# The last two experts' first product as seven block products, in a reordered tail

## The chip, the cores and the metric

One core of a Trainium2 chip runs the whole program. The metric is the device time of one execution in microseconds (us); the time of a kernel is the median of its runs. Engines are named as in the profile: PE is TensorE (its weight loads are PEld), DVE is VectorE, ACT is ScalarE, POOL is GpSimd, SP is SyncE, which only issues transfers here. PSUM is the memory that PE accumulates in, SBUF the one that holds operands.

## The reference

An attention over 4 x 8 heads of 768 positions and 64 elements comes first: queries and keys are assigned to 16 clusters, a query sees the keys of its own cluster, and the result is gathered into x with 3072 rows of 512. Then a mixture of 8 experts, with 384 rows for each:

```
logits = x @ w_gate                     # 3072 x 8
order = np.argsort(-logits.flatten())   # greedy: best pair first
# a row goes to an expert if the row is free and the expert has under 384 rows
for e in range(8):
    h = np.maximum(x[mask_e] @ w1[e], 0.0)   # 384 x 512 @ 512 x 1024
    out[mask_e] = h @ w2[e]                  # 384 x 1024 @ 1024 x 512
```

The first product and the second of an expert have the same number of multiplications. Everything that the change touches is the first product of two experts.

## The kernel before, in words

**Order.** The steps of the program stand in two tables of text, `ATT_ORDER` (line 21) for the attention and `FFN_ORDER` (line 181) for the experts. A step is a name and numbers, `hid,5,2,0,1`, and the loop at line 1503 calls the function `f_hid(5, 2, 0, 1)` for it. Each engine runs its own instructions in the order in which the table issues them, and waits on semaphores for operands that other engines write. No loop and no scheduler decides anything beyond the table.

**Precision.** A number is kept as two fp16 parts, an upper part and a lower part (what is left of it). A product is three PE passes: upper by upper, upper by lower, lower by upper.

**An expert p.** Its rows are ranked and picked: `rank` (1294) is a product on PE that counts the marks `mk` made by `gt` and `ge` (1283) on DVE; `scan`, `addr`, `stt0`, `pm`, `ph`, `pl`, `ohl`, `ohh`, `ohv` (1298 to 1351) turn the counts into one-hot tiles on DVE; `col` (1358, three products on PE), `pb0`, `pb1` (DVE), `rep` (1369, PE), `pi` and `idx` (1372, 1375, DVE) give the list of 384 rows. `gx` (1422, POOL) gathers 128 rows by that list and `xt` (1426, SP) transposes them into `xgt`; there are three of each. `es2`, `upe`, `lt`, `upd` (1312 to 1321) take the rows out of the scores for the next expert.

**Its weights.** `w_load` (1394, 1397, SP) brings w1 and w2 in eight pieces of 512 KB into `wr`; for each piece `wsc` (1408) scales it and `whi` (1411) takes the upper half on ACT, and `wlo` (1418) subtracts to get the lower half on POOL, each 128x1024 elements.

**Its products.** `hid` (function `triple`, 1450) makes the first product: 8 row blocks of the hidden layer x 4 blocks of the depth x 3 passes = 96 matmuls, each of 128x128 weights by 128x384 columns. Each finished block of 128x384 in PSUM goes through `rel` (1479, ACT, relu and upper half `hh`) and `hlo` (1482, DVE, lower half `hl`). `out` (1492) makes the second product: 3 groups of 128 rows x 8 x 3 = 72 matmuls of 512 columns (expert 7's third group is cut into 384 and 128 columns). `oev` (1496, ACT) copies a group out of PSUM and `sc` (1499, POOL) scatters it to the result. `hid` and `out` share five PSUM buffers, all called `pf`.

Before the change the products of experts 5, 6 and 7 follow each other whole: 96 `hid`, then 72 `out`, for each expert. Work for the next expert's rows and weights is strewn between them.

## Time and profile before

| | us |
|---|---|
| runs | 675.21, 675.34, 676.72 |
| median | 675.34 |
| the profiled execution | 676.28 |
| its span | 674.5 |
| PE busy | 634.6 (94%) |
| POOL busy | 514.3 (76%) |
| DVE busy | 500.0 (74%) |
| ACT busy | 420.8 (62%) |

The span is the time between the first and the last record of the trace; what the execution takes beyond it (676.28 - 674.5) lies outside. Busy shares are means over the whole span: attention and experts have different limits, so the stretch that the change touches has to be looked at by itself. The mean granted clock of PE over the span is 0.979 of its upper level. A matmul's busy time includes the way through the array and overlaps the next one; what a matmul costs in a row of matmuls is the distance from its start to the next start.

### The profile page before, as it was taken

The page shows a single profiled execution, that of the slowest core. Times are in us where ns is not written, and L with a number is a line of the kernel's source. Part 1 is how long each engine was busy: PE and PEld are TensorE (multiplying, and loading weights), DVE is VectorE, ACT ScalarE, POOL GpSimd, SP SyncE. Part 2 cuts the span into 40 slices and gives each one's busy share as a digit, 9 for nine tenths or more (in the row PEclk, how much of TensorE's full clock was granted, in tenths as well). Part 3 has the DMA queues.
Part 4 walks back from the last instruction along what each step waited for, and adds up shares of the span by engine and source line. Part 5 has one row for each costly group of instructions (what it writes and reads, how often), then busy time and mean ns, then how long its engine had stood idle before and what let it go on. Part 6 is the DMA issues. An engine that isn't in the chain of part 4 may idle for free. (4 is left out here: it accounts for less than half of the span.)

```text
span 674.5 us, 19513 instructions
## 1 busy us (share of the span) xinstructions
PE 634.6 (94%) x8154; PEld 427.0 (63%) x8154; DVE 500.0 (74%) x1092; ACT 420.8 (62%) x558; POOL 514.3 (76%) x451
## 2 busy tenths in 40 slices
...
GB/s 233 144 144 194 204 171 215 135 164 196 197 131 161 201 143 114 149 91 74 28 28 97 25 171 172 284 96 280 203 191 223 181 231 161 242 297 212 47 1 48
DMA packets 175451, 105.85 MB, mean 157 GB/s; under 512 B 135426, under 2 KB 160002, under 8 KB 175362
## 3 DMA queue, kind: packets, MB, share of 16 engines
...
q14 instruction: 25, 0.20, 0.1%
...
## 5 line engine op out<-in xcount | busy, mean ns | idle before, releaser
L841 POOL TENSOR_TENSOR rt<-pt 128x768 f16<-128x768 f32 x180 | 277.6, 1563 | 27.3 <-ACT pt L833 26.5
L833 ACT ACTIVATE pt<-sc 128x768 f32<-128x768 f32 x192 | 149.8, 811 | 93.6 <-PE sc L830 74.6
L791 DVE TENSOR_REDUCE mxs<-sc 128x1 f32<-128x768 f32 x192 | 176.0, 950 | 17.7 <-PE sc L787 17.2
L1450 PE MATMUL pf<-xgt,w1h 128*128 128x384 f16 (+1 forms) x640 | 130.1, 295 | 0.4 <-DVE xgt L751 0.4
L855 PE MATMUL av<-vh,rt 128*128 128x65 f16 x1152 | 120.6, 193 | 1.8 <-POOL rt L841 1.7
L852 PE MATMUL av<-vh,pt 128*128 128x65 f16 x1152 | 120.7, 194 | 1.1 <-DVE xb L885 1.1
L854 PE MATMUL av<-vl,pt 128*128 128x64 f16 x1152 | 120.4, 192 | 0.0
L854 PEld LDWEIGHTS <-pt 128*128 128x128 bf16 x1152 | 105.7, 98 | 8.9 <-issue 1.8
L852 PEld LDWEIGHTS <-pt 128*128 128x128 bf16 x1152 | 106.2, 97 | 7.4
L855 PEld LDWEIGHTS <-rt 128*128 128x128 f16 x1152 | 105.3, 97 | 2.1 <-POOL rt L841 2.0
L826 PE MATMUL sc<-qbt,kbt 99*128 99x384 f16 x384 | 94.5, 327 | 1.3 <-DVE mxs L791 0.7
L830 PE MATMUL sc<-qat,kat 128*128 128x384 f16 x384 | 94.5, 327 | 0.0
L787 PE MATMUL sc<-kbt,qbt 80*128 80x384 f16 x384 | 89.5, 327 | 2.8 <-ACT qbt L749 0.6
L1450 PE MATMUL pf<-xgt,w1l 128*128 128x384 f16 (+1 forms) x320 | 89.6, 294 | 0.0
L1408 ACT ACTIVATE wr<-wr 128x1024 f32<-128x1024 f32 x64 | 66.7, 1046 | 28.3 <-DVE cs L1344 20.8
L1450 PEld LDWEIGHTS <-w1h 128*128 128x128 f16 x640 | 58.0, 98 | 29.9 <-DVE xgt L751 1.0
L1492 PE MATMUL pf<-w2l,hh 128*128 128x512 f16 (+2 forms) x200 | 73.5, 370 | 0.0
L1492 PE MATMUL pf<-w2h,hl 128*128 128x512 f16 (+2 forms) x200 | 73.4, 370 | 0.0
L1492 PE MATMUL pf<-w2h,hh 128*128 128x512 f16 (+2 forms) x200 | 73.3, 370 | 0.0
L1418 POOL TENSOR_TENSOR w1l<-wr,w1h 128x1024 f16<-128x1024 f32 x32 | 67.4, 2133 | 4.5 <-ACT w1h L1411 4.3
L1418 POOL TENSOR_TENSOR w2l<-wr,w2h 128x1024 f16<-128x1024 f32 x32 | 67.7, 2138 | 3.9 <-ACT w2h L1411 3.5
L1482 DVE SCALAR_TENSOR_TENSOR hl<-pf,hh 128x384 f16<-128x384 f32 x56 | 30.9, 553 | 46.4 <-ACT hh L1479 46.0
...
## 6 DMA issues: line engine op xcount, KB each, us to landing
...
xg<-xrow,idx POOLq DMA_INDIRECT x24, 6.8
```

The source lines that it names most:

```text
L787: nc.tensor.matmul(p[:, half, :S // 2], QBT[u][:D + C, i, :], KBT[u][:D + C, h * J + half * 3:h * J + half * 3 + 3, :], start=True, stop=True)
L791: nc.vector.tensor_reduce(mxs[u % 3][:, i:i + 1], MP.pop((u, i))[:, :, :S // 2], axis=AX.XY, op=OP.max)
L826: nc.tensor.matmul(ps[:, half, :S // 2], KBT[u][:ER + 3, s, :], QBT[u][:ER + 3, cs, :], start=True, stop=False)
L830: nc.tensor.matmul(ps[:, half, :S // 2], KAT[u][:, s, :], QAT[u][:, cs, :], start=False, stop=True)
L833: nc.scalar.activation(pts[(u * 12 + s // 2) % RP][:, s % 2], MP.pop((u, "b", s))[:, :, :S // 2], AF.Exp, scale=ESC)
L841: (nc.vector if e == "D" else nc.gpsimd).tensor_sub(rts[x][:, s % 2], p.rearrange("p a b -> p (a b)"), hi_view(pts[x])[:, s % 2])
L852: nc.tensor.matmul(o[:, j, :D + 1], hi[:, js], VH[u][:, s, :D + 1], start=(kt == 0 and j == 0), stop=False, skip_group_check=True)
L854: nc.tensor.matmul(o[:, j, :D], hi[:, js], VL[u][:, s, :], start=False, stop=False, skip_group_check=True)
L855: nc.tensor.matmul(o[:, j, :D + 1], r[:, js], VH[u][:, s, :D + 1], start=False, stop=(kt == J - 1), skip_group_check=True)
L1418: nc.gpsimd.tensor_sub(lo, wrs[c], hi)
L1450: nc.tensor.matmul(o, (w1l if i == 2 else w1h)[x][:, c, fs], xgt[x][:, h + int(i == 1), ts], start=(first and i == 0), stop=(last and i == ...
L1492: nc.tensor.matmul(PS["o", p, g], (hl if i == 2 else hh)[x][:, f, g * P:(g + 1) * P], (w2l if i == 1 else w2h)[x][:, f, ds], start=(f == 0 ...
```

## The change

For experts 6 and 7 the first product is computed by Strassen's scheme in Winograd's form. The weights of an expert are taken as 2x2 blocks (depth 2 x 256, hidden 2 x 512) and its rows as 2x2 blocks (depth 2 x 256, rows 2 x 192). Seven products of blocks take the place of eight. Each product is issued as two steps `sp` of 12 matmuls (2 blocks of the hidden layer x 2 of the depth x 3 passes) with 192 columns: 14 steps and 168 matmuls for an expert, where 96 with 384 columns were.

New steps for each of the two experts:

- `sS` (8, DVE): sums and differences of weight blocks, 128x512 in fp32, both inputs in SBUF.
- `sh` (14, ACT) and `sl` (14): upper and lower halves of the blocks and of their sums, 128x512; of `sl` 10 are on POOL and 4 on DVE for expert 6, 4 on POOL and 10 on DVE for expert 7.
- `tx` (1, DVE, 128x1536), `tt` (4, DVE, 128x384), `th` (4, ACT), `tl` (4, DVE): sums of the rows' blocks and their halves.
- `cy` (6, ACT) copies the running sum Z out of PSUM, `ad` (6, DVE) adds such a copy to Y or X; `re` (8, ACT) and `hs` (8, DVE) take the place of `rel` and `hlo`.

Gone for each of them: the 4 `whi` and 4 `wlo` of w1. The `wsc`, the loads, the gathers, transposes, second products and scatters stay in number. From the step `c3,6` on (the choice of expert 6) the whole table is written in another order, also for expert 5: its `hid` and `out` steps no longer follow each other whole, and those of experts 5 and 6 are put between the `sp` of 6 and 7. Two lines of the table, then the code (line numbers in the changed file are lower by 8 up to `triple` and higher by 85 from `f_hid` on):

```diff
-c3,6 hid,5,1,3,2 ei,6 hid,5,2,0,0 mq,6 hid,5,2,0,1 reg,6 rel,5,1 hid,5,2,0,2 gt,6 hid,5,2,1,0 ge,6 hid,5,2,1,1 hlo,5,1
+c3,6 hid,5,1,3,2 ei,6 hid,5,2,0,0 mq,6 hid,5,2,0,1 reg,6 gt,6 hid,5,5,0,0 w_load,6,0 hid,5,4,0,0 hid,5,4,0,1
+hid,5,4,0,2 hid,5,4,1,0 rel,5,1 hlo,5,1 ge,6 rank,6 es2,6 upe,6 hid,5,4,1,1 hid,5,4,1,2 hid,5,4,2,0 hid,5,4,2,1
...
@@ -1470,6 +1462,99 @@
         else:
             V.scalar_tensor_tensor(hl[0][s_], PS["h", g, fh], 0.0, hh[0][s_], op0=OP.max, op1=OP.subtract)
 
+    SH = F // 2
+    sxh, sxl = (ex.tile([P, 3, 2, SH], F16, name=n) for n in ("sxh", "sxl"))
+    tsp = ex.tile([P, 4, 2, 2, CAP // 2], F16, name="tsp")
+    zcs = [ex.tile([P, 2, CAP // 2], F32, name=f"zc{i}") for i in range(4)]
+    sms = [ex.tile([P, 2, CAP // 2], F32, name=f"sm{i}") for i in range(2)]
+    HOME = {"A11": 0, "A12": 1, "S2": 2, "S1": 0, "S3": 1, "S4": 2, "A22": 3}
+    RAW = {"A11": (0, 0), "A12": (0, 2), "A22": (1, 2), "S1": (1, 2), "S2": (0, 0), "S3": (1, 0), "S4": (0, 2)}
+    SUMS = {1: ((1, 2), (1, 0), (1, 2), OP.add), 3: ((1, 0), (0, 0), (1, 0), OP.subtract),
+            2: ((0, 0), (1, 2), (0, 0), OP.subtract), 4: ((0, 2), (0, 2), (0, 0), OP.subtract)}
+    half = (slice(0, CAP // 2), slice(CAP // 2, CAP))
+
+    def sraw(r, k):
+        return wrs[r[1] + k][:, r[0] * SH:(r[0] + 1) * SH]
+
+    def shome(p, b, k):
+        h = HOME[b]
+        if b in ("A11", "A12", "S2"):
+            return sxh[:, h, k, :], sxl[:, h, k, :]
+        c, o = 2 * (h // 2) + k, (h % 2) * SH
+        return w1h[p % 2][:, c, o:o + SH], w1l[p % 2][:, c, o:o + SH]
+
+    def f_sh(p, b, k):
+        nc.scalar.activation(shome(p, b, k)[0], sraw(RAW[b], k), AF.Copy)
+
+    def f_sl(p, b, k, e):
+        hi, lo = shome(p, b, k)
+        (V if e == "D" else nc.gpsimd).tensor_sub(lo, sraw(RAW[b], k), hi)
+
+    def f_sS(p, n, k):
+        o, a, b, op = SUMS[n]
+        V.tensor_tensor(sraw(o, k), sraw(a, k), sraw(b, k), op=op)
+
+    def sxf(p):
+        return hh[p % 2].rearrange("p f n -> p (f n)").bitcast(F32).rearrange("p (c n) -> p c n", c=DC)
+
+    def stt(p, n):
+        t = hl[p % 2].rearrange("p f n -> p (f n)").bitcast(F32).rearrange("p (t c n) -> p t c n", t=4, c=2)
+        return t[:, n - 1]
+
+    def f_tx(p):
+        x = xgt[p % 2].rearrange("p (c w) n -> p c w n", w=2)
+        V.tensor_tensor(sxf(p), x[:, :, 0, :], x[:, :, 1, :], op=OP.add)
+
+    def f_tt(p, n):
+        x = sxf(p)
+        b = lambda j, l: x[:, 2 * j:2 * j + 2, half[l]]
+        l, r = {1: (b(0, 1), b(0, 0)), 2: (b(1, 1), stt(p, 1)), 3: (b(1, 1), b(0, 1)), 4: (b(1, 0), stt(p, 2))}[n]
+        V.tensor_tensor(stt(p, n), l, r, op=OP.subtract)
+
+    def f_th(p, n):
+        nc.scalar.activation(tsp[:, n - 1, :, 0, :], stt(p, n), AF.Copy)
+
+    def f_tl(p, n):
+        V.tensor_tensor(tsp[:, n - 1, :, 1, :], stt(p, n), tsp[:, n - 1, :, 0, :], op=OP.subtract)
+
+    PROD = {1: ("A11", (0, 0)), 2: ("A12", (1, 0)), 3: ("S4", (1, 1)), 4: ("A22", 4), 5: ("S1", 1), 6: ("S2", 2), 7: ("S3", 3)}
+    ACC = {1: "Z", 6: "Z", 5: "Z", 3: "Z", 2: "Y", 7: "X", 4: "X"}
+
+    def f_sp(p, n, q):
+        blk, t = PROD[n]
+        z, first, last = ACC[n], n in (1, 2, 7), n in (3, 2, 4)
+        if first:
+            PS[z, q] = pff.tile([P, 2, CAP // 2], F32, name="pf")
+        for m in range(2):
+            fs = slice((2 * q + m) * P, (2 * q + m + 1) * P)
+            for k in range(2):
+                h, l = shome(p, blk, k)
+                if isinstance(t, int):
+                    xh, xl = tsp[:, t - 1, k, 0, :], tsp[:, t - 1, k, 1, :]
+                else:
+                    xh, xl = (xgt[p % 2][:, 2 * (2 * t[0] + k) + w, half[t[1]]] for w in range(2))
+                for i, (a, b) in enumerate(((h, xh), (h, xl), (l, xh))):
+                    nc.tensor.matmul(PS[z, q][:, m, :], a[:, fs], b, start=(first and m == 0 and k == 0 and i == 0),
+                                     stop=(last and m == 1 and k == 1 and i == 2), skip_group_check=True)
+
+    def f_cy(p, i, q, s):
+        nc.scalar.activation(zcs[s], PS["Z", q], AF.Copy)
+
+    def f_ad(p, z, q, s, o):
+        V.tensor_tensor(sms[o], PS[z, q], zcs[s], op=OP.add)
+
+    def sout(t, p, b, q):
+        i, l = b // 2, b % 2
+        f = 4 * i + 2 * q
+        return t[p % 2][:, f:f + 2, half[l]]
+
+    def f_re(p, b, q, o):
+        nc.scalar.activation(sout(hh, p, b, q), PS["Z", q] if o is None else sms[o], AF.Relu)
+
+    def f_hs(p, b, q, o):
+        V.scalar_tensor_tensor(sout(hl, p, b, q), PS["Z", q] if o is None else sms[o], 0.0, sout(hh, p, b, q),
+                               op0=OP.max, op1=OP.subtract)
+
     def f_hid(p, f, c, i):
         if c == 0 and i == 0:
             PS["h", p, f] = pff.tile([P, CAP], F32, name="pf")
@@ -1487,13 +1572,13 @@
     def f_out(p, g, f, i, w=2):
         ds = span(w)
         if f == 0 and i == 0:
-            PS["o", p, g] = pff.tile([P, ds.stop - ds.start], F32, name="pf")
+            PS["o", p, g, w] = pff.tile([P, ds.stop - ds.start], F32, name="pf")
         x = p % 2
-        nc.tensor.matmul(PS["o", p, g], (hl if i == 2 else hh)[x][:, f, g * P:(g + 1) * P], (w2l if i == 1 else w2h)[x][:, f, ds],
+        nc.tensor.matmul(PS["o", p, g, w], (hl if i == 2 else hh)[x][:, f, g * P:(g + 1) * P], (w2l if i == 1 else w2h)[x][:, f, ds],
                          start=(f == 0 and i == 0), stop=(f == FC - 1 and i == 2))
 
     def f_oev(p, g, w=2):
-        nc.scalar.activation(ots[(3 * p + g) % 4][:, span(w)], PS["o", p, g], AF.Copy, scale=1.0 / (SX * SW * SW))
+        nc.scalar.activation(ots[(3 * p + g) % 4][:, span(w)], PS["o", p, g, w], AF.Copy, scale=1.0 / (SX * SW * SW))
 
     def f_sc(p, g):
         nc.gpsimd.indirect_dma_start(out=out, out_offset=bass.IndirectOffsetOnAxis(ap=idx[p % 4][:, g:g + 1], axis=0),
...
```

The first place, on DVE, is the ranking of expert 6, at the head of the reordered part (`mk` are the marks that `gt` and `ge` write, `L` the scores, `tot` what `scan` makes of `rank`, `pk` small tables, `hl` the lower halves of expert 5's hidden blocks). Before:

```order
L1280 TENSOR_TENSOR mq<-m_7976,pk 128x24
L1283 SCALAR_TENSOR_TENSOR mk<-pk,pc,mq 128x24 x2
L1482 SCALAR_TENSOR_TENSOR hl_8036<-pf,hh_8034 128x384
L1312 TENSOR_SCALAR pk<-pk 128x8
L1318 SCALAR_TENSOR_TENSOR L<-pk,L 128x192
L1298 SCALAR_TENSOR_TENSOR tot<-pc,mk 128x48
L1301 TENSOR_TENSOR pk<-tot,pc 128x48
L1305 SCALAR_TENSOR_TENSOR pk<-pk,mk 128x48
L1482 SCALAR_TENSOR_TENSOR hl_8036<-pf,hh_8034 128x384
L1308 TENSOR_REDUCE pk<-pk 128x24
L1325 TENSOR_SCALAR pk<-pk 128x24
L1328 TENSOR_SCALAR pk<-pk 128x24
```

After:

```order
L1272 TENSOR_TENSOR mq<-m_7976,pk 128x24
L1275 SCALAR_TENSOR_TENSOR mk<-pk,pc,mq 128x24
L1567 SCALAR_TENSOR_TENSOR hl_8036<-pf,hh_8034 128x384
L1275 SCALAR_TENSOR_TENSOR mk<-pk,pc,mq 128x24
L1304 TENSOR_SCALAR pk<-pk 128x8
L1310 SCALAR_TENSOR_TENSOR L<-pk,L 128x192
L1290 SCALAR_TENSOR_TENSOR tot<-pc,mk 128x48
L1293 TENSOR_TENSOR pk<-tot,pc 128x48
L1297 SCALAR_TENSOR_TENSOR pk<-pk,mk 128x48
L1300 TENSOR_REDUCE pk<-pk 128x24
L1317 TENSOR_SCALAR pk<-pk 128x24
L1320 TENSOR_SCALAR pk<-pk 128x24
```

The lower half `hlo,5,1` now stands between the two marks instead of behind both, and the one that stood between `stt0` and `pm` has gone to a later place.

The second place, on DVE, is the row list of expert 7 (`cq`, `cs`, `pg`, `idx`: the steps `pb0`, `pb1`, `pi`, `idx`). Before:

```order
L1335 TENSOR_TENSOR ohv<-ohl,pk 128x384
L1362 TENSOR_TENSOR cq_8002<-pc,own_189 128x192
L1365 TENSOR_REDUCE cs_8003<-cq_8002 128x24
L1372 SCALAR_TENSOR_TENSOR pg<-pc,own_189 128x24
L1375 TENSOR_REDUCE idx_8010<-pg 128x3
L1482 SCALAR_TENSOR_TENSOR hl_8035<-pf,hh_8033 128x384 x8
```

After, from `tt` to the next `tt` of expert 6 (`sm` are the sums that `ad` writes, `tsp` the halves of the rows' sums, `w1l` and `wr` a lower half and the loaded weights):

```order
L1512 TENSOR_TENSOR hl_8035<-hh_8033 128x384
L1491 TENSOR_TENSOR w1l_8021<-wr_8013,w1h_8019 128x512
L1544 TENSOR_TENSOR sm_8050<-pf,zc_8046 128x384
L1364 SCALAR_TENSOR_TENSOR pg<-pc,own_189 128x24
L1367 TENSOR_REDUCE idx_8010<-pg 128x3
L1544 TENSOR_TENSOR sm_8051<-pf,zc_8047 128x384
L1518 TENSOR_TENSOR tsp<-hl_8035,tsp 128x2x192
L1491 TENSOR_TENSOR w1l_8021<-wr_8013,w1h_8019 128x512
L1512 TENSOR_TENSOR hl_8035<-hh_8033,hl_8035 128x384
```

`pi` and `idx` of expert 7 stood behind `pb1`, with only expert 6's and 7's lower halves to follow; now they stand between the additions and splits of expert 6's block products.

## Rows read from the trace of the kernel before

**Rows 1.** Windows: start:end, span, then busy us of PE, PEld, DVE, ACT, POOL, clock

```profile
636.79:652.39 15.60, 15.60 (x98) 9.39 (x96) 3.90 (x7) 4.03 (x8) 0.96 (x1) 1.00 0.05 18
652.39:668.20 15.81, 15.76 (x97) 8.37 (x95) 0.56 (x1) 2.19 (x5) 1.92 (x2) 1.00 0.09 34
577.36:668.20 90.84, 90.79 (x520) 48.91 (x517) 25.59 (x71) 46.80 (x65) 47.23 (x30) 1.00 0.49 152
```

**Rows 2.** Timeline of PE around the steps of experts 6 and 7: start, us, instruction

```profile
578.66 0.19 PE L1294 MATMUL pc<-mk,tri 128*128 128x48 bf16 x1
583.15 0.42 PE L1358 MATMUL pc<-ohh,ohv 128*128 128x192 f16 x3
583.41 0.33 PE L1450 MATMUL pf<-xgt,w1h 128*128 128x384 f16 x1
584.54 0.17 PE L1369 MATMUL pc<-cs,rep 128*128 128x24 f16 x1
...
601.06 0.41 PE L1358 MATMUL pc<-ohh,ohv 128*128 128x192 f16 x3
601.31 0.38 PE L1492 MATMUL pf<-w2l,hh 128*128 128x512 f16 x1
```

**Rows 3.** Timeline of DVE around expert 6's ranking: start, us, instruction

```profile
577.63 0.40 DVE L1283 SCALAR_TENSOR_TENSOR mk<-pk,pc,mq 128x24 bf16<-128x24 f32 x2
578.25 0.56 DVE L1482 SCALAR_TENSOR_TENSOR hl<-pf,hh 128x384 f16<-128x384 f32 x1 [0.21 <-ACT hh L1479]
578.72 0.23 DVE L1312 TENSOR_SCALAR pk<-pk 128x8 f32<-128x8 f32 x1
579.26 0.25 DVE L1298 TENSOR_TENSOR_SCAN tot<-pc,mk 128x48 f32<-128x48 f32 x1
...
580.25 0.56 DVE L1482 SCALAR_TENSOR_TENSOR hl<-pf,hh 128x384 f16<-128x384 f32 x1 [0.24 <-ACT hh L1479]
580.72 0.21 DVE L1308 TENSOR_REDUCE pk<-pk 128x24 int32<-128x48 f32 x1
581.41 0.56 DVE L1331 TENSOR_TENSOR ohl<-pk,loc 128x384 f16<-128x384 int32 x1
581.89 0.75 DVE L1351 TENSOR_TENSOR ohh<-pk,hic 128x576 f16<-128x576 int32 x1
```

**Rows 4.** Groups by line, 577.36 to 668.2 us: busy, mean ns, idle before

```profile
L1450 PEld LDWEIGHTS <-w1h 128*128 128x128 f16 x176 | 17.2, 98 | 11.6 <-issue 0.2
L1418 POOL TENSOR_TENSOR w1l<-wr,w1h 128x1024 f16<-128x1024 f32 x8 | 16.8, 2130 | 0.0
L1479 ACT ACTIVATE hh<-pf 128x384 f16<-128x384 f32 x23 | 11.2, 489 | 20.1 <-PE pf L1450 20.1
```

**Rows 5.** Timeline of DVE: two splits of v in the attention, one indicator later

```profile
84.11 1.75 DVE L656 SCALAR_TENSOR_TENSOR ka<-ld,ka 128x1536 f16<-128x1536 f32 x1
85.77 3.02 DVE L656 SCALAR_TENSOR_TENSOR vl<-ld,vh 128x1536 f16<-128x1536 f32 x1
...
533.17 0.96 DVE L1186 TENSOR_TENSOR ind<-pk,offs 128x768 bf16<-128x768 f32 x1
```

**Rows 6.** Timeline of POOL in the same two stretches

```profile
85.53 4.59 POOL L841 TENSOR_TENSOR rt<-pt 128x768 f16<-128x768 f32 x2 [2.35 <-ACT pt L833]
...
532.24 4.24 POOL L1418 TENSOR_TENSOR w2l<-wr,w2h 128x1024 f16<-128x1024 f32 x2
```

**Rows 7.** Operations of line 1186: min, median and max ns, first and last start

```profile
L1186 DVE TENSOR_TENSOR ind<-pk,offs x6: 956/958/958, 407.1 to 566.4; 128x768 bf16<-128x768 f32 x6
```

**Rows 8.** Timeline of PE in the attention: two products of 65 columns

```profile
210.24 0.19 PE L855 MATMUL av<-vh,rt 128*128 128x65 f16 x1
210.27 0.19 PE L852 MATMUL av<-vh,pt 128*128 128x65 f16 x1
```

**Rows 9.** Timeline of POOL: expert 7's last gather

```profile
606.89 0.95 POOL L1422 DMA_INDIRECT xg<-xrow,idx  x1 [0.30 <-issue]
```

**Rows 10.** Timeline of SP: expert 7's three transposes

```profile
610.85 4.71 SPq L1426 DMA_TRANSPOSE xgt<-xg  x3
```

More of the change, by code (lines that the diff above doesn't have):

```diff
@@ L367 @@
-hid,5,3,3,2 hid,5,4,0,0 ohl,6 w_load,6,5 hid,5,4,0,1 rel,5,3 hid,5,4,0,2 hid,5,4,1,0 ohh,6 hid,5,4,1,1 w_load,6,6
-hid,5,4,1,2 hid,5,4,2,0 hid,5,4,2,1 ohv,6 w_load,6,7 hid,5,4,2,2 hid,5,4,3,0 lt,6 col,6 wsc,6,0 upd,6 hid,5,4,3,1
-hid,5,4,3,2 pb0,6 hid,5,5,0,0 hid,5,5,0,1 hid,5,5,0,2 pb1,6 hid,5,5,1,0 rel,5,4 hlo,5,3 rep,6 hid,5,5,1,1 hid,5,5,1,2
-whi,6,0,C hid,5,5,2,0 pi,6 hid,5,5,2,1 hid,5,5,2,2 idx,6 hid,5,5,3,0 hlo,5,4 gx,6,0 hid,5,5,3,1 hid,5,5,3,2
-hid,5,6,0,0 wsc,6,1 b,7,0 hid,5,6,0,1 hid,5,6,0,2 hid,5,6,1,0 b,7,1 hid,5,6,1,1 hid,5,6,1,2 gx,6,1 b,7,2 hid,5,6,2,0
@@ L377 @@
-out,5,0,4,2 out,5,0,5,0 out,5,0,5,1 w_load,7,0 wlo,6,2,C rank,7 out,5,0,5,2 scan,7 out,5,0,6,0 xt,6,0 wsc,6,4
-out,5,0,6,1 addr,7 out,5,0,6,2 stt0,7 out,5,0,7,0 pm,7 out,5,0,7,1 ph,7 out,5,0,7,2 whi,6,4,C pl,7 out,5,1,0,0 ohl,7
-xt,6,1 out,5,1,0,1 out,5,1,0,2 wlo,6,3,C ohh,7 out,5,1,1,0 out,5,1,1,1 oev,5,0 out,5,1,1,2 ohv,7 out,5,1,2,0 xt,6,2
-out,5,1,2,1 wsc,6,5 out,5,1,2,2 out,5,1,3,0 out,5,1,3,1 out,5,1,3,2 out,5,1,4,0 sc,5,0 whi,6,5,C out,5,1,4,1
-w_load,7,1 out,5,1,4,2 out,5,1,5,0 w_load,7,2 out,5,1,5,1 out,5,1,5,2 wsc,6,6 wlo,6,4,C out,5,1,6,0 w_load,7,3
@@ L382 @@
-out,5,1,6,1 out,5,1,6,2 out,5,1,7,0 out,5,1,7,1 wsc,7,0 out,5,1,7,2 out,5,2,0,0 out,5,2,0,1 out,5,2,0,2 oev,5,1
-out,5,2,1,0 wlo,6,5,C w_load,7,4 col,7 out,5,2,1,1 whi,6,6,C pb0,7 out,5,2,1,2 out,5,2,2,0 pb1,7 out,5,2,2,1
-out,5,2,2,2 out,5,2,3,0 whi,7,0,C rep,7 out,5,2,3,1 pi,7 out,5,2,3,2 sc,5,1 idx,7 out,5,2,4,0 w_load,7,5 out,5,2,4,1
-wsc,6,7 out,5,2,4,2 out,5,2,5,0 out,5,2,5,1 out,5,2,5,2 gx,7,0 out,5,2,6,0 wsc,7,1 out,5,2,6,1 out,5,2,6,2 out,5,2,7,0
-out,5,2,7,1 gx,7,1 out,5,2,7,2 whi,6,7,C hid,6,0,0,0 hid,6,0,0,1 hid,6,0,0,2 hid,6,0,1,0 hid,6,0,1,1 hid,6,0,1,2
```

112 lines of the change are left out of this document (59 added, 53 removed).

## The prediction

> **What bounds the kernel now.** Three views were read, in this order. The windows first: the page's totals (PE busy 94%) average over attention and experts, so the stretch from 577.36 us, where the reordered part of the table begins, to PE's last product has to stand alone. There PE is busy in 90.79 of 90.84 us, DVE in 25.59, ACT in 46.80 and POOL in 47.23, with the clock at 1.00, its upper level of 2.4 GHz [rows 1]. So PE bounds this stretch, and what an edit takes off PE comes off the time, as long as nothing makes PE wait. The same view gives the first product of expert 7 alone: 15.60 us [rows 1], 96 matmuls, so 0.1625 each from start to start. The timeline of PE is read second, for what a matmul of 192 columns costs and where the steps of experts 6 and 7 stand [rows 2]. The timeline of DVE is read third, for the chain that PE will wait for [rows 3]. The sum is made against the profiled execution, 676.28, which stands 0.94 above the median of 675.34; the median is predicted as 0.94 below the sum.
>
> **The products.** Removed: 2 x 15.60 = 31.20 us of PE. Added: 2 x 168 matmuls of 192 columns. Their price is bounded from both sides. Half of the 0.1625 for 384 columns is 0.0813. Three 128x192 matmuls start at 601.06 and the next instruction at 601.31, 0.0833 each; another three take from 583.15 to 583.41, 0.0867 each [rows 2]; both times they stand between other shapes. I take 0.0825, nearest to the first two, since the new ones stand in steps of twelve. 168 x 0.0825 = 13.86, so 1.74 saved for an expert and **-3.48** for both; the ends are -3.88 and -2.06. Seven products for eight would suggest an eighth of 31.20, 3.90; the rest is the fixed part of each matmul, of which there are now more.
>
> **The ranking of expert 6.** Before, `rank` starts at 578.66 and `rep` at 584.54, 5.88 apart [rows 2]. Between them lie 33 `hid` (5.36), `col` (0.26) and `rank` itself (some 0.06), 5.68 in all, so PE lost 0.20 there. After, `rank` has the same 8 `hid` ahead of it, but on DVE its second mark stands behind `hlo,5,1`, which waits for ACT's relu until 578.25 and lets the next operation start at 578.72 [rows 3]. The pair of marks took 0.40 [rows 3]; one takes some 0.24, so `ge` ends at 578.96 and `rank` starts at about 579.02: 0.36 lost. Then DVE: `es2` and `upe` take 579.26 - 578.72 = 0.54 and follow `ge` (0.20 to the next start), so `scan` starts at 579.46. From `scan` to `pm` it was 1.46, of which 0.47 were a lower half and 0.24 its wait [rows 3]; that one has moved away, so `pm` starts at 580.21. `ohl` comes 0.69 later [rows 3], at 580.90; `ohl` and `ohv` 0.48 each, `ohh` 0.75: ready at 582.61, and `col` can start at 582.67. PE has 17 `hid` between `rank` and `col` where 27 were, and is there at 579.02 + 0.06 + 2.76 = 581.84: 0.83 lost. Then `col` and 16 `hid` (6 before) bring `rep` to 585.53, **+1.0** against before, with no wait left for `rep`. Ends: 0.6, if `hlo,5,1` comes 0.4 sooner, and 1.3. The rows behind `rep` lose nothing: the gathers of expert 6 come later than before, but 67 `out` and 32 `hid` of expert 5 stand ahead of the first block product.
>
> **The row list of expert 7.** Ahead of the step `sp,6,3,0` DVE has to do, after `rep,7`: `pi` and `idx` (0.4, small like the tables of the ranking), an `ad` and a `tl` (0.47 each, as a lower half of 128x384), and a split `sl` of 128x512, 4/3 of 0.47 = 0.62 by columns; with 0.2 for the way from PE, 2.2. PE has one `out` (0.1625 x 4/3 = 0.22) and two `sp` (24 x 0.0825 = 1.98) in that time, 2.20. The two are even: 0 to 0.3 lost here, up to 2.1 if a POOL operation of 2130 ns [rows 4] holds one of these up. With the bank that `hid,5,7` needs from a lower half of expert 5 (0.05) I take **+0.3** for all waits besides the ranking.
>
> **What is added beside PE.** DVE gets 60 operations more than it loses: at 0.47 for 128x384, 0.62 for 128x512 and 1.75 for 128x1536 [rows 3, 5] some 35 us, so 60 of 87. ACT gets 28 `sh`, 8 `th` and 12 `cy` for 8 `whi`; at 489 ns for 128x384 [rows 4] some 16 us more, so 62 of 87. POOL trades 8 `wlo` of 2130 ns [rows 4] for 14 halves of that, slightly less. None of the three passes PE, so their totals cost nothing; that holds only while they run ahead of it. Where the cover is gone, the price is the whole operation. The end is the same: the last block of 128 columns, its copy and its scatter follow PE as before.
>
> **The sum.** -3.48 + 1.0 + 0.3 = -2.2, so 676.28 becomes 674.1, and the median 673.2. A measurement of this kernel can tell 0.3%, 2.0 us, from no change; the forecast lies on that line.
>
> **Rivals.**
> *No waits at all.* Expert 5's relu and lower half come sooner than I reckon because ACT and DVE hold fewer of them at that time, or the waits are made up because PE would have waited later anyhow: 675.34 - 3.48 = 671.9, or 671.5 with the other end of the price. For it: 33 `hid` still stand between `rank` and `rep`. Against it: the DVE chain itself is longer than 17 `hid`.
>
> *Expert 7's rows come late.* From the last gather's start to the end of the transposes it is 610.85 + 4.71 - 606.89 = 8.7 us [rows 9, 10]. Counting PE's steps by the spacings above, `rep,7` falls at 612.4 and the first block product of expert 7 at 631.8. On POOL the last gather has two subtractions of 2.13 and two gathers of 0.95 ahead of it and starts at about 620; 628.6 with its transposes. But on SP two of them stand behind a weight load, which waits until `wlo,6,6` on POOL has freed its buffer. If that subtraction comes one operation later than I count, the 3 us are used up, and another 2.1 come onto the path: -2.2 + 2.1, so 675.3 (674 to 677).
>
> *VectorE and GpSimd shut each other out, and the kernel is slower.* A split of 128x1536 with two inputs in SBUF took 1.75 us at 84.11 and 3.02 at 85.77, where a POOL subtraction had started at 85.53 [rows 5, 6]. In the tight part, from 605 to 648 us, POOL has three `wlo` and four `sl`, 3 x 2.13 + 4 x 1.07 = 10.7 us, beside DVE's sums and splits of both experts, most with two inputs in SBUF. From 2.2 us of such holds on the path on, the kernel is no faster than before; with half of the 10.7 it is 673.2 + 5.3 = 678.5, with all 683.9. Against it: the operation of line 1186, also with two inputs in SBUF, ran at 533.17 in the midst of two `wlo` and took 0.96 [rows 5, 6], as the fastest of its six did, 956 ns [rows 7]; and the new `sl` on POOL are `wlo` of half the length. The Trainium skill ("SBUF — State Buffer", section "SBUF: two separate sides") says that a VectorE operation with two SBUF inputs and a GpSimd operation that reads SBUF exclude each other for the whole instruction. By that rule this rival would be the likeliest; the trace agrees at 85.77 and does not at 533.17.
>
> *The narrow matmuls wait for their own weights.* A weight load takes 98 ns [rows 4], more than 0.0825; at 0.098 each 168 take 16.46, 0.86 more than the 96 did, and the sum is +1.7 + 1.3 = +3.0: 678.3. Against it: matmuls of 65 columns with a load each start 0.03 apart [rows 8].
>
> **How the numbers follow.** Forecast 0.52, around 673.2 (672.3 to 674.5), half on each side of the 2.0 us; no waits 0.13; expert 7's rows late 0.18; exclusion 0.12; own weights 0.03; something else, slower, 0.02. Faster by over 0.3%: 0.26 + 0.13, and 0.01 of the late rows: 0.40. Slower: 0.12 + 0.03 + 0.02 and 0.01 of the late rows: 0.18. The rest, 0.42, is within 0.3%. The range runs from the low end of no waits, 671.4, to the upper end of the late rows, 677.0; exclusion and own weights lie above it and are most of what is left out.
>
> **What would show it.** The `sp` steps with twelve matmuls in 0.99 us; a PE wait of about 0.4 before line 1286 (`rank`) and 0.8 before line 1350 (`col`) near 579 and 582; no idle PE of over 0.3 from there to the end; splits and sums on DVE of 0.6 to 0.75 us, beside POOL too. Wrong would be: `sp` steps of 1.04 or more, DVE operations of 1.5 us or more beside a POOL subtraction, or PE idle ahead of line 1537 (`sp`) or of the `out` behind it by over 1 us in all.

## The result and the profile after

| | before | after |
|---|---|---|
| median of 22 runs each, us | 676.40 | 679.99 |
| the profiled execution, us | 676.28 | 679.9 |
| PE busy, us | 634.6 | 632.7 |
| DVE busy, us | 500.0 | 548.4 |
| ACT busy, us | 420.8 | 436.5 |
| POOL busy, us | 514.3 | 519.1 |

The ratio of after to before is 1.0052, with the interval 1.0041 to 1.0063. The kernel is slower, by 3.5 us, where 2.2 us less was forecast. The time lies above the range.

The account starts at the last small product ahead of the reordered steps, line 1213 before (574.75 us) and 1205 after (575.17). PE's last product starts 93.18 us later before, 95.55 after: +2.37. The last scatter starts at 668.74 and at 672.36: +3.20 from there.

The first view is that of line 1537, the new products: minimum, median and maximum ns of one matmul in its largest group (a busy time, not a distance from start to start):

```profile
L1537 PE MATMUL pf<-tsp,w1h x96: 242/246/246, 613.6 to 656.1; 128*128 128x192 f16 x96
```

From start to start the `sp` matmuls take 0.082 or 0.083 us, 0.0825 in the mean. The 336 of them without the waits are 27.73 us, for 31.20 before: **-3.47**.

The second view is PE's waits from 570 to 680 us (total, times, longest):

```profile
PE pf L1577 <- DVE hl L1555: 2.1, 2, 1.4
PE pf L1537 <- DVE tsp L1518: 1.5, 1, 1.5
PE pc L1350 <- DVE ohh L1343: 0.9, 1, 0.9
...
```

The third is PE's timeline at these places. A gap is counted from start to start, less the usual spacing of the shape ahead of it (0.213 for 512 columns, 0.0825 for 192, 0.1625 for 384), and so comes out some 0.2 larger than the bracket:

```profile
578.92 0.33 PE L1442 MATMUL pf<-xgt,w1h 128*128 128x384 f16 x1
579.44 0.18 PE L1286 MATMUL pc<-mk,tri 128*128 128x48 bf16 x1 [0.19 <-DVE mk L1275]
...
583.31 0.33 PE L1350 MATMUL pc<-ohh,ohv 128*128 128x192 f16 x2 [0.90 <-DVE ohh L1343]
...
618.51 0.38 PE L1577 MATMUL pf<-w2l,hh 128*128 128x512 f16 x1
619.65 0.39 PE L1577 MATMUL pf<-w2h,hl 128*128 128x512 f16 x1 [0.76 <-DVE hl L1555]
...
621.30 0.25 PE L1537 MATMUL pf<-tsp,w1h 128*128 128x192 f16 x1
623.06 0.24 PE L1537 MATMUL pf<-tsp,w1h 128*128 128x192 f16 x1 [1.52 <-DVE tsp L1518]
...
638.37 0.38 PE L1577 MATMUL pf<-w2l,hh 128*128 128x512 f16 x1
640.11 0.39 PE L1577 MATMUL pf<-w2h,hl 128*128 128x512 f16 x1 [1.35 <-DVE hl L1555]
```

The gaps are 0.35 ahead of `rank`, 1.06 ahead of `col`, 0.14 ahead of `rep`, then 0.92, 1.68 and 1.52 at 619, 622 and 639 us, and 0.37 at 654: 6.04, where the same count gives 0.16 before. So PE gains 3.47 and loses 5.88, +2.41, where +2.37 was measured. The other 0.83 lie behind PE, in the scatters.

What made PE wait is seen in DVE's groups from 577.97 to 672 us (busy, mean ns). One line stands here twice, once with its inputs in SBUF and once with one in PSUM:

```profile
L1555 DVE SCALAR_TENSOR_TENSOR hl<-sm,hh 128x384 f16<-128x384 f32 x12 | 12.0, 1014 | 2.0 <-ACT hh L1552 1.8
...
L1518 DVE TENSOR_TENSOR tsp<-hl,tsp 128x384 f16<-128x384 f32 x8 | 8.4, 1060 | 0.0
L1544 DVE TENSOR_TENSOR sm<-pf,zc 128x384 f32<-128x384 f32 x12 | 6.6, 549 | 0.2
...
L1555 DVE SCALAR_TENSOR_TENSOR hl<-pf,hh 128x384 f16<-128x384 f32 x4 | 2.1, 548 | 1.0 <-ACT hh L1552 1.0
```

With `pf`, a PSUM tile, as one input, 128x384 takes 0.55 (lines 1544 and 1555). With both in SBUF the mean is 1.01 and 1.06. DVE's timeline and POOL's show where the excess arises:

```profile
616.06 3.53 DVE L1555 SCALAR_TENSOR_TENSOR hl<-sm,hh 128x384 f16<-128x384 f32 x2
...
620.45 2.56 DVE L1518 TENSOR_TENSOR tsp<-hl,tsp 128x384 f16<-128x384 f32 x1
```

```profile
616.04 0.96 POOL L1414 DMA_INDIRECT xg<-xrow,idx  x1 [0.30 <-issue]
617.03 2.14 POOL L1410 TENSOR_TENSOR w2l<-wr,w2h 128x1024 f16<-128x1024 f32 x1
619.33 1.10 POOL L1414 DMA_INDIRECT xg<-xrow,idx  x1 [0.16 <-issue]
620.44 2.14 POOL L1410 TENSOR_TENSOR w2l<-wr,w2h 128x1024 f16<-128x1024 f32 x1
```

The second half of the first row began at 616.55 and ended at 619.6, behind the subtraction. The `tl` of 620.45 is the one that PE waits for at 623.06. The three large gaps, 4.12 us together, stand behind such held operations. The third stands behind an `hs` of 639.50 with its own 0.55, queued behind an `sS` of 1.53 and a `tx` of 2.71 (1.75 by [rows 5]) beside two `sl` on POOL (first DVE, then POOL):

```profile
634.23 1.53 DVE L1495 TENSOR_TENSOR wr<-wr,wr 128x512 f32<-128x512 f32 x1
635.68 2.71 DVE L1506 TENSOR_TENSOR hh<-xgt 128x1536 f32<-128x1536 f16 x1
```

```profile
633.92 1.30 POOL L1491 TENSOR_TENSOR w1l<-wr,w1h 128x512 f16<-128x512 f32 x1 [10.03 <-ACT w1h L1487]
635.17 1.60 POOL L1491 TENSOR_TENSOR sxl<-wr,sxh 128x512 f16<-128x512 f32 x1
```

Here the two engines took turns: the `sS` ended at 635.76, 0.54 behind the first `sl`, and the second `sl` took 1.60, where most of them took 1.16.

The scatters, on POOL's timeline:

```profile
665.38 0.99 POOL L1584 DMA_INDIRECT out_dram<-ot,idx  x1 [2.58 <-ACT ot L1581]
668.88 0.96 POOL L1584 DMA_INDIRECT out_dram<-ot,idx  x1 [2.52 <-ACT ot L1581]
672.36 0.96 POOL L1584 DMA_INDIRECT out_dram<-ot,idx  x1 [2.51 <-issue]
```

They stand 3.50 and 3.47 apart. Before, the last two stood 4.87 apart:

```profile
663.87 0.96 POOL L1499 DMA_INDIRECT out_dram<-ot,idx  x1 [4.27 <-ACT ot L1496]
668.74 0.96 POOL L1499 DMA_INDIRECT out_dram<-ot,idx  x1 [3.91 <-ACT ot L1496]
```

Now the third group's copy is done sooner than the scatter ahead of it lets go.

### The profile page after: what moved, and what is told of

Same layout as the page of the kernel before. It is cut to its first block, busy times and chain, and to the rows that moved or that the text cites. A ratio compares the mean times of both kernels' runs of the same rounds, so it can differ in the third digit from the quotient of the medians.

```text
span 678.1 us, 19882 instructions
## 1 busy us (share of the span) xinstructions
PE 632.7 (93%) x8298; PEld 435.7 (64%) x8298; DVE 548.4 (81%) x1152; ACT 436.5 (64%) x598; POOL 519.1 (77%) x457
## 3 DMA queue, kind: packets, MB, share of 16 engines
q8 instruction: 65, 1.06, 0.7%
## 5 line engine op out<-in xcount | busy, mean ns | idle before, releaser
L1442 PE MATMUL pf<-xgt,w1h 128*128 128x384 f16 (+1 forms) x512 | 98.9, 287 | 0.4 <-DVE xgt L743 0.4
L1577 PE MATMUL pf<-w2h,hl 128*128 128x512 f16 (+2 forms) x200 | 72.0, 370 | 2.1 <-DVE hl L1555 2.1
L1442 PE MATMUL pf<-xgt,w1l 128*128 128x384 f16 (+1 forms) x256 | 68.4, 287 | 0.0
L1442 PEld LDWEIGHTS <-w1h 128*128 128x128 f16 x512 | 45.5, 98 | 21.5 <-DVE xgt L743 1.0
L1577 PEld LDWEIGHTS <-hh 128*128 128x128 f16 x400 | 37.1, 97 | 34.3 <-ACT w1h L1403 0.8
L1414 POOL DMA_INDIRECT xg<-xrow,idx x24 | 24.7, 1027 | 39.8 <-DVE idx L1367 26.9
```

The lines of the kernel that those rows point to most:

```text
L1442: nc.tensor.matmul(o, (w1l if i == 2 else w1h)[x][:, c, fs], xgt[x][:, h + int(i == 1), ts], start=(first and i == 0), stop=(last and i == ...
L1577: nc.tensor.matmul(PS["o", p, g, w], (hl if i == 2 else hh)[x][:, f, g * P:(g + 1) * P], (w2l if i == 1 else w2h)[x][:, f, ds], start=(f = ...
```

## The experiments

Two theories stood at the start. One: the held operations on DVE are the cost, since VectorE and GpSimd shut each other out. The rival: the order of the table is, with operations queued ahead of those that PE needs.

**pool_writes_only.** Seven of POOL's subtractions become two writes each.

```diff
+        elif (p, c) in ((6, 4), (6, 6), (6, 7)):
+            [nc.gpsimd.memset(lo, 0.0) for _ in range(2)]
...
-        (V if e == "D" else nc.gpsimd).tensor_sub(lo, sraw(RAW[b], k), hi)
+        if e == "P" and p == 7:
+            [nc.gpsimd.memset(lo, 0.0) for _ in range(2)]
+        else:
+            (V if e == "D" else nc.gpsimd).tensor_sub(lo, sraw(RAW[b], k), hi)
```

> The changed kernel, but seven of GpSimd's subtractions between 605 and 653 us (three wlo of expert 6, four sl of expert 7) are two memsets of the same tile each: GpSimd stays busy for about as long and reads no SBUF; the lower halves concerned are zero. Theory (exclusion): the held operations go back to their own length, hs at 616.6 from 3.04 to 0.55 us, tl at 620.4 from 2.56 to 0.55, the sum sS at 634.2 from 1.53 to 0.69, and PE's stalls of 0.92 (at 618.5), 1.68 (at 621.3) and 1.52 us (at 638.4) vanish: 4.1 us faster than the changed kernel, about 0.5 us under the kernel before. Rival (VectorE simply has too much work in this order, with GpSimd no cause): the stalls stay within 0.5 us of what they were, and the time within 1 us of the changed kernel.

679.24 against 676.52, ratio 1.0036 (1.0021 to 1.0050). The operations concerned fell to 0.55 (`hs`), 0.56 (`tl`), 0.69 (`sS`) and 1.75 (`tx`), and the three gaps were gone. The `tl` (620.69) and two later `sS` (645.63) ran beside writes and kept their length; the `sS` and `tx` of the third gap stood beside an idle POOL, because the writes in place of the `sl` read nothing, so no longer waited for ACT, and were done by 627.7. But the time hardly fell. On ACT, the first scaling of expert 7's weights now waits, and `hh`, which PE needs, is queued behind it (PE: 0.56 and 0.93 at 630 and 631):

```profile
627.23 1.06 ACT L1400 ACTIVATE wr<-wr 128x1024 f32<-128x1024 f32 x1 [3.81 <-DMA wr<-in_moe_w_dram]
...
630.46 0.51 ACT L1557 ACTIVATE hh<-sm 128x384 f16<-128x384 f32 x1
```

And two subtractions that were left on POOL, back to back from 648.62 to 652.84, held a `tl` for 4.66 us and PE for 1.9 behind it.

**before_with_probes.** The kernel before, with operations on DVE that nobody waits for: `pa`, plain with two fp32 inputs; `pb`, `pc`, `pd`, with repeated indices or int32; `pe`, with one input.

```diff
+    def f_pe():
+        V.tensor_scalar(px[2], px[0], 1.0, None, op0=OP.mult)
...
-hid,6,1,2,2 wlo,6,6,C hid,6,1,3,0
+pa pb hid,6,1,2,2 wlo,6,6,C hid,6,1,3,0
```

> The kernel before with 32 idle probes on VectorE between 605 and 640 us, beside GpSimd's subtractions, 128x512 elements each, on tiles of their own: pa subtracts two fp32 tiles read in full; pb compares two fp32 tables, both read with a repeated (broadcast) index, as line 1186 does; pc is pb in int32; pd subtracts a repeated table from a full tile; pe scales one fp32 tile. Reading of the exclusion that every operation with two SBUF inputs falls under it: pa, pb, pc and pd take up to 2.1 us longer beside a subtraction, pe takes its own length. Second reading, which would explain why line 1186 was not held: pa is held, pb and pc are not. If there is no exclusion here: all keep their own length, pa 0.69 us. A held probe may also show as a subtraction longer than 2.15 us.

694.21 us. DVE's timeline, then POOL's:

```profile
613.06 17.08 DVE L1524 TENSOR_SCALAR px<-px 128x512 f32<-128x512 f32 x1
...
634.12 0.42 DVE L1524 TENSOR_SCALAR px<-px 128x512 f32<-128x512 f32 x1
...
636.36 2.58 DVE L1512 TENSOR_TENSOR px<-px,px 128x512 f32<-128x512 f32 x1
```

```profile
612.13 1.00 POOL L1498 DMA_INDIRECT out_dram<-ot,idx  x1 [2.69 <-ACT hh L1478]
613.15 2.15 POOL L1417 TENSOR_TENSOR w2l<-wr,w2h 128x1024 f16<-128x1024 f32 x1
...
625.67 4.19 POOL L1417 TENSOR_TENSOR w2l<-wr,w2h 128x1024 f16<-128x1024 f32 x2
```

One operation with one input, a `pe` of 0.42 by itself, was held for 17.08 us, which no reading had expected. It began 0.09 us ahead of the first of eight subtractions, which followed back to back to 629.9, and it was not let in between two of them. PE lost 9.76 us behind it. A `pb` at 636.36 (2.58 for 0.68) and a `pc` at 644.24 (3.23 for 0.68) were held too, so repeated indices alone do not free an operation; no `pa` or `pd` came to stand beside a subtraction. So the exclusion exists in the kernel before too, which had no such operation on DVE at these places.

**three_order_edits.** Both marks together, `hs,6,2,1,1` ahead of `tx,7`, and some of the third group's products later, to let the second group's scatter go sooner.

```diff
-reg,6 gt,6 hid,5,5,0,0 w_load,6,0
+reg,6 gt,6 ge,6 hid,5,5,0,0 w_load,6,0
...
-tx,7 tt,7,1 tt,7,2 out,6,1,4,0 out,6,1,4,1 sh,7,S1,0 out,6,2,4,2 out,6,1,4,2 hs,6,2,1,1
+hs,6,2,1,1 tx,7 tt,7,1 tt,7,2 out,6,1,4,0 out,6,1,4,1 sh,7,S1,0 out,6,2,4,2 out,6,1,4,2
```

> The changed kernel with three edits of its table: the mark ge of expert 6 ahead of hlo,5,1 and six more hid ahead of col (PE waited 0.35 and 1.06 us there); hs,6,2,1,1 ahead of the sum tx of expert 7 (PE waited 1.52 us for it at 638.4); seven products of the last block behind the second block's last product, so that its scatter starts sooner (the last scatter waited 0.8 us for the landing of the one before). Theory (these waits lie on the path one behind the other): each goes at its own place, 1.2 + 1.2 + 0.8 = 3.2 us faster than the changed kernel. Rival (time won early is lost at the next stall, where a held operation of VectorE does not move with PE): the ranking's 1.2 us come back as a longer stall at 618 to 622, and no more than 2 us are won.

681.95, ratio 1.0075 (1.0050 to 1.0100). The wait of `rank` went, that of `col` fell to 0.15, and `rep` waited 1.1 instead. The gap at 639 split in two (0.54 and 0.85). The scatter of the second group came 5.8 us after the first, not sooner. Order alone does not cure it.

**hs_from_psum.** The sums for `re` and `hs` are left in PSUM, so that `hs` has one input there.

```diff
-        V.tensor_tensor(sms[o], PS[z, q], zcs[s], op=OP.add)
+        V.tensor_tensor(sms[o] if z == "X" and s < 2 else PS[z, q], PS[z, q], zcs[s], op=OP.add)
```

> The changed kernel, but ad writes the sums for three of the four result blocks back to PSUM where they came from, and re and hs read them there: the 8 operations hs concerned have one input in SBUF. Theory (exclusion acts on operations with two SBUF inputs): none of these hs is longer than 0.6 us beside a subtraction (two thirds of a us to 3.04 us in the changed kernel), the stall of 0.92 us at 618.5 goes, those behind tl (1.68) and behind the sum at 634 (1.52) stay: 0.9 us faster. Rival (a PSUM buffer kept longer makes the next product wait): new waits of PE before an sp or out that opens a buffer, and no gain or a loss of 1 to 2 us.

684.30, ratio 1.0104 (1.0059 to 1.0150). The `hs` concerned took 0.55 to 0.6 beside POOL: an input in PSUM does free an operation. But the hold moved to the next one, an `sl` of 3.08 at 618.47, and the PSUM buffers came free later:

```profile
638.97 0.50 PE L1537 MATMUL pf<-xgt,sxh 128*128 128x192 f16 x2 [3.05 <-DVE hl L1558]
```

After this wait the windows view gives a granted clock of 0.50, the lower level of 1.2 GHz, from 639.0 to 642.3, and 1.00 behind it.

**subtractions_on_vector.** Ten of POOL's subtractions on DVE instead: the four `sl` and two of the `wlo` from above, and the four `wlo` of expert 7's w2.

```diff
+        elif v == "D":
+            V.tensor_sub(lo, wrs[c], hi)
...
-tt,7,4 sl,7,S1,1,P out,6,1,6,2 out,6,1,7,0 out,6,0,7,2 oev,6,0 sl,7,S2,1,P
+tt,7,4 sl,7,S1,1,D out,6,1,6,2 out,6,1,7,0 out,6,0,7,2 oev,6,0 sl,7,S2,1,D
```

> The changed kernel, but ten of GpSimd's subtractions after 615 us (wlo,6,6, wlo,6,7, wlo,7,4 to wlo,7,7 and the last four sl of expert 7) are on VectorE, the two of expert 6 behind hs steps that are more urgent, and w_load,7,6 is behind the transposes of expert 7's rows. GpSimd then subtracts nothing between 615 and the end; VectorE gets some 10 us more work of its own. Theory (the holding, not the amount of work, made PE wait): no VectorE operation after 615 us is more than 0.1 us over its own length, the stalls at 618.5 and 621.3 go (2.6 us), and what the run with write-only GpSimd showed remains: the ranking (1.4) and 1 to 1.5 us for the relu of expert 6 behind the scaling of expert 7's weights on ScalarE. 2 to 3 us faster than the changed kernel, 0.995 to 1.000 of the changed kernel's ratio. Rival (VectorE is simply full): the sums and halves queue behind the added 10 us, PE waits over 1 us before out steps for hl or w2l, and nothing is won.

679.37, ratio 1.0050 (1.0025 to 1.0076). From 607 us on no operation on DVE was held any more (two short holds, at 599.0 and 605.6, stayed, and PE does not wait behind them). Still PE lost 5.6 us in all: 1.55 in the ranking as before, 4.1 in other places than in after. Its longest waits from 570 us on:

```profile
PE pc L1349 <- DVE ohh L1342: 0.9, 1, 0.9
PE pf L1538 <- DVE tsp L1519: 0.8, 2, 0.6
PE pf L1578 <- DVE hl L1556: 0.8, 1, 0.8
PE pf L1578 <- ACT hh L1553: 0.8, 1, 0.8
...
```

So there is a second limit.

**subtractions_and_order.** This kernel with the order edits, and `re,6,2,0,0` ahead of expert 7's scaling.

```diff
+re,6,2,0,0 hs,6,2,0,0 wsc,7,3 sh,7,A22,1 sl,7,A22,1,D
-wsc,7,3 sh,7,A22,1 sl,7,A22,1,D
```

> The run subtractions_on_vector, with edits of the table for the other waits: ge of expert 6 ahead of hlo,5,1, four more hid ahead of col, and the four steps b,7 behind pb1 (ranking, 1.4 us); re,6,2,0,0 ahead of the scaling wsc,7,3 that waits for a transfer (1 to 1.5 us); hs,6,2,1,1 ahead of tx,7; seven products of the last block behind the second block's last (the end, 0.8 us). Theory (all of the loss is waits with a name, the products do save 3.6 us): 4 to 6 us faster than the changed kernel, so 0.995 to 1.001 of the kernel before. Rival (the chains are so close to PE that a wait removed only uncovers the next one, which does not move with PE): less than 2 us faster than the changed kernel, with new waits of over 0.5 us between 625 and 665.

681.00, ratio 1.0060 (1.0040 to 1.0079). The gaps at 629 and 630 went, and others of 1.37 and 1.22 came behind 641. ACT and DVE were late as a whole there; who goes first among them changes little.

**before_with_table_probes.** Is the form of line 1186 free of holds, as [rows 5] had it? The kernel before with one-hot tables made beside POOL: `qa` from fp32, `qb` from int32, both to bf16.

```diff
+    def f_qb():
+        V.tensor_tensor(wide(po), pn[0][:, :32, None].to_broadcast([P, 32, 16]), pn[1][:, None, :16].to_broadcast([P, 32, 16]), op=OP.is_ge)
```

> The kernel before with five probes on VectorE between 608 and 625 us, 128x512, on tiles of their own, beside back-to-back GpSimd subtractions: twice qa (two fp32 tables with repeated index, written as bf16, the form of line 1186), twice qb (the same from int32), once qc (the same from fp32, written as fp32, the form that was held for 1.9 us in before_with_probes). If the width of what is written decides: qa and qb take 0.7 us each though GpSimd subtracts, qc is held until GpSimd has a gap (up to 8 us). If chance of timing let line 1186 through: qa is held as well, until the first gap of GpSimd.

689.75 us. `qb` was held for 17.82 us, from 611.59, behind the eight subtractions that began at 612.17. The `qa`, the form of line 1186, stood beside no subtraction, so the run says nothing of it. But the traces of all 13 kernels do: 62 operations of line 1186 began in the midst of a subtraction of POOL (with at least 0.25 us of it to go), and all took their 0.96. So its row was no accident, and it was no proof that tables are free.

**weights_in_place.** subtractions_on_vector without the four loads of expert 7's w1, to see whether late weights are the second limit. In after, SP issues these loads from 610.13 to 618.7 (with two of w2 among them), since their buffers hold expert 6's sums until then: the first waits 8.1 us for an `sl` of expert 6 on DVE. Before, it issues them from 592.60 to 600.4. SP's timeline, before and after:

```profile
592.60 0.35 SPq L1394 DMA_DIRECT2D wr<-in_moe_w_dram  x1
...
598.88 1.56 SPq L1394 DMA_DIRECT2D wr<-in_moe_w_dram  x3
```

```profile
610.13 0.99 SPq L1386 DMA_DIRECT2D wr<-in_moe_w_dram  x2
614.45 1.02 SPq L1389 DMA_DIRECT2D wr<-in_moe_w_dram  x2
615.90 2.79 SPq L1386 DMA_DIRECT2D wr<-in_moe_w_dram  x2
```

```diff
+        if p == 7 and c < 4:
+            return
...
-        nc.scalar.activation(wrs[c], wrs[c], AF.Copy, scale=SW)
+        nc.scalar.activation(wrs[c], wrs[c], AF.Copy, scale=1.0 if p == 7 and c < 4 else SW)
```

> The run subtractions_on_vector, but expert 7's first weights are not loaded (its four loads of w1 are left out and its scaling multiplies by 1): it splits and sums what expert 6 left in the buffers, so its output rows are wrong in value, and ScalarE no longer waits at 621 to 626 us for transfers issued only at 610 to 618 (592 to 600 in the kernel before, since Strassen keeps expert 6's sums in those buffers). Theory (behind the holding lies a second limit: expert 7's weights come late, ScalarE and VectorE then work without a gap from 626 to 645 and PE waits for them): the stalls of 0.92 and 0.93 at 629 and 630.5 and those of 0.25 and 0.74 at 641 to 643 vanish; 2 to 3 us faster than subtractions_on_vector, a ratio to the kernel before of 1.000 to 1.002. Rival (ScalarE and VectorE are full with or without the weights): the stalls only shift, under 0.7 us won.

674.46 against 675.62, ratio 0.9988 (0.9970 to 1.0007). By the two ratios this is some 4 us less than subtractions_on_vector. Behind the ranking one gap of 0.20 is left; PE loses 1.77 in all, 1.57 of it in the ranking. Without the wait for the loads, ACT's work on expert 7 spreads over both stretches. Windows of weights_in_place, then of subtractions_on_vector (start:end, span, busy us of PE, PEld, DVE, ACT, POOL):

```profile
605.60:626.00 20.40, 20.40 (x193) 16.31 (x192) 18.40 (x34) 17.48 (x31) 7.40 (x6) 1.00 0.54 168
626.00:645.00 19.00, 19.00 (x166) 14.09 (x164) 18.13 (x31) 16.13 (x30) 2.73 (x2) 1.00 0.25 84
```

```profile
605.60:626.00 20.40, 19.95 (x196) 16.35 (x195) 16.45 (x30) 11.50 (x23) 8.96 (x8) 1.00 0.75 238
626.00:645.00 19.00, 16.81 (x110) 9.43 (x108) 16.96 (x28) 18.45 (x31) 2.02 (x1) 1.00 0.35 91
```

With late weights ACT has 11.50 in the first and 18.45 of 19.00 in the second, where PE loses 2.19.

**strassen_expert_7_only.** Both causes taken away in a kernel that computes everything: expert 6 keeps its 96 `hid` and the order of before, expert 7 alone has the seven products, with its sums strewn between expert 6's steps, and the subtractions from 608 us on are on DVE. Against the kernel before:

```diff
-hid,6,1,2,2 wlo,6,6,C hid,6,1,3,0 xt,7,0
+sl,7,A11,0,D sl,7,A11,1,D hid,6,1,2,2 wlo,6,6,D hid,6,1,3,0 xt,7,0
```

> The block products for expert 7 alone. Up to expert 6's second product the table is that of the kernel before, with the sums and splits of expert 7 strewn in behind expert 6's lower halves (all sl, and the wlo from 608 us on, are on VectorE); from the first block product on it is that of the changed kernel. Expert 7's weights are loaded as early as before, the ranking is as before, VectorE was nearly idle there (4.46 us busy of 31.19). Theory (the products pay where there is room beside them; all of the loss came from chains that had none): half of the saving, 1.8 us, less up to 0.8 us for the last scatter: 0.997 to 0.999 of the kernel before, no PE wait over 0.4 us after 577 us. Rival (the block products always bring waits of their own size): PE waits of 1.5 us or more before or between the sp steps, 1.000 to 1.003.

674.26 against 675.62, ratio 0.9979 (0.9970 to 0.9989): faster than before by 1.4 us. PE's waits are empty, and from `rank` to its last product it takes 87.54 us (576.40 to 663.94), where it took 89.27: -1.73, and one expert's products were to give 1.74. To the last scatter it is -0.95 only; the scatters stand 3.47 apart again.

**strassen_7_tail.** That kernel with four products of the third group moved behind the second.

```diff
-out,7,2,2,0,0 out,7,2,2,1,0 out,7,2,2,2,0 re,7,3,1,1
+re,7,3,1,1
...
+out,7,2,2,0,0 out,7,2,2,1,0 out,7,2,2,2,0 out,7,2,3,0,0 out,7,2,1,0,1
```

> The kernel of strassen_expert_7_only, with four products of expert 7's third group (rows 256 to 383) moved behind the last product of the second group, so that the first and second groups are copied and scattered earlier. The scatters of strassen_expert_7_only began at 658.60, 662.07 and 665.53, each 3.47 after the one before, the last one some 0.8 later than its data. Theory (a scatter cannot begin before the one ahead of it has landed, 3.5 us, and this is what the end costs): the second scatter comes some 0.65 us sooner, the last one waits less, and the time falls by 0.3 to 0.7 us, ratio to before about 0.997. Rival (a larger distance brings a longer landing wait, as the 5.3 us in three_order_edits and subtractions_and_order): the last scatter waits as long or longer, ratio 0.998 or above it.

674.75 against 676.25, ratio 0.9974 (0.9961 to 0.9988). From `rank` (579.50) the last scatter starts 88.48 us later, 0.65 sooner than in strassen_expert_7_only (89.13). The intervals of the two ratios overlap, so the medians cannot tell them apart. The profile bears the theory out: the chain of three scatters starts sooner and its steps keep their length (661.04, 664.52, 667.98).

**strassen_7_pool_subtractions.** strassen_expert_7_only with ten subtractions back on POOL.

```diff
-hid,6,1,2,2 wlo,6,6,D hid,6,1,3,0
+hid,6,1,2,2 wlo,6,6,C hid,6,1,3,0
...
-tt,7,4 sl,7,S1,1,D out,6,1,6,2 out,6,1,7,0 out,6,0,7,2 oev,6,0 sl,7,S2,1,D
+tt,7,4 sl,7,S1,1,P out,6,1,6,2 out,6,1,7,0 out,6,0,7,2 oev,6,0 sl,7,S2,1,P
```

> The kernel of strassen_expert_7_only, with ten subtractions put back from VectorE to GpSimd: six wlo of 128x1024 (2.1 us each) and four sl of 128x512 (1.1 us each), 17 us of GpSimd. In strassen_expert_7_only PE has no gap, and VectorE is busy in 18.2 of the 20.4 us from 605.6 to 626, which this edit relieves by as much as it loads GpSimd. Theory (VectorE and GpSimd shut each other out, and this alone costs PE time): although VectorE has less to do, several of its sums and halves take 1.5 us or more beside a GpSimd subtraction, PE waits behind them for 1 us or more in all, and the kernel is at least 0.8 us slower than strassen_expert_7_only, ratio to before 0.999 or above. Rival (the holds are there but the room that expert 7 alone has hides them, or the loads of expert 7 were the only cause): no PE gap over 0.3, the same time as strassen_expert_7_only within 0.4 us.

681.07 against 676.25, ratio 1.0080 (1.0059 to 1.0102). PE has one gap. DVE, POOL and PE there:

```profile
645.53 5.21 DVE L1560 SCALAR_TENSOR_TENSOR hl<-sm,hh 128x384 f16<-128x384 f32 x1 [0.31 <-ACT hh L1557]
650.84 0.56 DVE L1549 TENSOR_TENSOR sm<-pf,zc 128x384 f32<-128x384 f32 x1
```

```profile
644.96 1.12 POOL L1589 DMA_INDIRECT out_dram<-ot,idx  x1 [0.15 <-issue]
646.11 4.20 POOL L1415 TENSOR_TENSOR w2l<-wr,w2h 128x1024 f16<-128x1024 f32 x2
```

```profile
651.45 0.48 PE L1542 MATMUL pf<-tsp,w1h 128*128 128x192 f16 x2 [3.94 <-DVE sm L1549]
```

An `hs` of 0.55 began beside a scatter's issue, 0.58 us ahead of two `wlo`, and was held for 5.21, through both; the `ad` behind it frees the PSUM tile that PE needs. PE lost 4.10 there. Then its clock stood at 0.52 from 651.45 to 654.4, which cost another 1.35 by the spacings (11 matmuls of 192 columns at 0.160 and three wider ones). Together 5.45; from `rank` (577.33) to the last scatter (671.96) it is 94.63, 5.50 more than in strassen_expert_7_only. That is the exclusion by itself, with expert 6 as before.

## Why the prediction was wrong

**The products**: right. 0.0825 was taken and 0.0825 measured; -3.47 for -3.48.

**The ranking of expert 6**: right in mechanism and near in size. The waits were put at 0.36 and 0.83 and measured 0.35 and 1.06, with 0.14 more for `rep`: 1.39 over the 0.16 before, where 1.0 was taken and 1.3 was the upper end.

**What is added beside PE**: this step failed. "None of the three passes PE, so their totals cost nothing; that holds only while they run ahead of it." The condition did not hold, and totals were the wrong thing to ask. DVE's added operations do not have the lengths of rows that stood alone. With two inputs in SBUF beside POOL they took up to 3.04 for 0.55. ACT's total was right (15.7 us more, for 16); DVE's was 48.4 for 35, and 12.7 of that are holds. "The price is the whole operation" was too low as well: behind the 128x1024 subtractions the price was all that POOL still had to do without a pause.

**The rival** that VectorE and GpSimd shut each other out named what the new operations met. Half of 10.7, 5.3, was its price, and 4.1 of PE's gaps stand behind held operations; its 678.5 is 3.2 over the median before, where 3.5 was measured. That its time fits so well is partly luck, since nearly as much is lost without the holds (next paragraph). It was given 0.12 because of one row, line 1186 at 533.17 [rows 5, 6], against another, line 656 at 85.77, that showed the hold in the very form of the new operations, two inputs in SBUF that are read in full. The nearest row should have decided: in the 13 traces all 37 of the change's operations of that form (`sS`, `hs`, `sl`, `tl`, `tx`, `tt`) that began in the midst of a subtraction were held, while the 62 of line 1186, which compares two small tables with repeated indices, were not; and of 164 with 128x384 and one input in PSUM none was. By the Trainium skill ("SBUF — State Buffer", section "SBUF: two separate sides") a VectorE operation with two SBUF inputs and a GpSimd one that reads SBUF block each other for a whole instruction. The traces agree in form (5.21 at 645.53, 0.55 with an input in PSUM), but not for line 1186, and not in length: the 5.21 went through two GpSimd operations and the 17.08 through eight.

**The row list of expert 7**: "+0.3 for all other waits" was 4.5 (0.92, 1.68, 1.52 and 0.37). The rows themselves were not late: their transposes ended at 629.0, where 628.6 was counted. What was late is what I did not follow on SP: the loads of expert 7's weights, 12 to 18 us later than before, since `sS` keeps expert 6's sums in `wr`. This is a second limit of nearly the same size, hidden behind the first: of the 6.04 that PE loses, 5.6 are still lost without the holds, and 1.8 without the late loads as well. That is why pool_writes_only and subtractions_on_vector, which take away holds alone, won 0 to 1 us. The order edits, the rival among the theories for the cure, won nothing by themselves.

**"The end is the same"**: failed by 0.83. Faster last products do not reach the end, since the last three scatters follow 3.5 us apart.

The sum as measured: -3.47 + 5.88 + 0.83 = +3.24, where +3.20 was measured from line 1205 on; 0.42 more arose ahead of it, where the two programs are alike.
